# GpSimd work, narrowing steps and gate steps placed anew around the half experts of an attention, mixture and feed-forward kernel

## The chip, the cores and the metric

One NeuronCore of a Trainium2 chip runs the whole program. The metric is the device time of one execution in microseconds (us); 1 us is 1000 ns. The engines are TensorE (PE in the profile, with its weight loads as PEld), VectorE (DVE), ScalarE (ACT), GpSimd (POOL) and the queue that issues DMAs (SP). Each engine works through its own instructions in the order in which the code writes them.

## The reference

```python
# attention: 2 batches, 8 heads, 768 tokens, 64 wide; a window of 128 and 4 sink tokens
a = softmax(where(keep, q @ k.T / 8, -1e9)); x = a @ v          # x: 1536 x 512
# mixture: 8 experts, w1[e] 512 x 1024, w2[e] 1024 x 512
P = exp(x @ w_gate - max)
for _ in range(8):
    P /= P.sum(1, keepdims=True) + 1e-09
    P /= P.sum(0, keepdims=True) + 1e-09
    P *= N / E
for e in range(E):
    out += P[:, e:e+1] * (maximum(x @ w1[e], 0) @ w2[e])
# last layer: w_in 512 x 2048, w_out 2048 x 512
h = out @ w_in; result = (h - tanh(h)) @ w_out
```

## The kernel before

All products run as three matmuls of float32r halves: an operand is cast to a high half (ScalarE, in `split_step` L588), and a subtraction (L591) leaves the low half. The mixture is cut into 32 **half experts**: 2 batches of 768 tokens times 8 experts times 2 halves of the 1024 inner columns. The code counts them with `u`, from 0 to 31, in the loop of `mixture`, and so does the text.

The order of one half expert is written out by hand in `order`. First come the **first products** (`1a` to `3b`, 14 steps of six 384-column matmuls, a fast scheme with seven factors for each of two quartets a and b), with the steps `g0` and `g1` among them. Then come the **second products**: `g2`, `G0`, `G1`, `G2` (six 512-column matmuls each) and `A3`, `A4`, `A5` (twelve each). Second products of token tile n land in a PSUM tile `pg`; there are three of them, so `A5` writes into the one that `G2` left, after VectorE has added it to the accumulator `xa` (the instruction with the scalar `prob`, L939). That addition is called xa2 below, those of `G0` and `G1` xa0 and xa1, and so on to xa5.

Beside the matmuls, each half expert prepares weights for the next one:

- First weights. GpSimd forms sums of loaded blocks in `st` (`sum_next`, L553, two times four instructions). ScalarE casts them in four parts at `g2`, `G0`, `G1`, `G2`, and VectorE subtracts each part one step later (`pending`). Parts 1 and 3 have 1024 columns, parts 2 and 4 have 768. They go to `w1b`.
- Second weights. ScalarE casts two tiles of 1024 columns at `A3` and `A4`; GpSimd subtracts both at the head of the next half expert (`w2_steps`, `step(G)`), in front of the sums. They go to `w2b`.
- Narrowing. The weights of the last layer are converted in 32 pieces by eight VectorE instructions each (`narrow_piece`, tiles `n`, L686 to L701). A half expert takes up to ten such steps, from `u` = 2 on, not in `u` = 15.
- Gates. The normalisation of P (`gates`) runs in `u` = 0 and 1: each step of the generator is a group of small VectorE instructions with one TensorE product `pc`.

ScalarE copies results of first products out of PSUM (`p1`, `u2`, `u3`, L813) so that later factors can be added there.

Of the kernel before, what the change touches and what calls it, by code (L numbers as in the profile page):

```python
# [12 lines left out]
ALU = mybir.AluOpType  # L13
# [9 lines left out]
NI = S // P  # L23
# [18 lines left out]
class Kernel:  # L42
# [187 lines left out]
    def attention_narrow(self, ctx):  # L230
# [7 lines left out]
        ps_t = ctx.enter_context(tc.tile_pool(name="ps_t", bufs=2, space=PSUM))  # L238
        ps_k = ctx.enter_context(tc.tile_pool(name="ps_k", bufs=1, space=PSUM))
        ps_x = ctx.enter_context(tc.tile_pool(name="ps_x", bufs=1, space=PSUM))  # L240
        units = B * NP
# [130 lines left out]
        inputs = self.first_inputs()  # L372
        load_v(0)
        for t in range(T + 5):
# [32 lines left out]
            if t >= 10 and first:  # L407
                later.extend(x for x in [first.pop(0)()] if x)
            if 29 <= t < 29 + NI:
                self.gate_logits(t - 29, ps_t, "t")  # L410
            if t >= 29 and inputs:
                later.extend(x for x in [inputs.pop(0)()] if x)
# [293 lines left out]
    def gates(self, gp):  # L706
# [16 lines left out]
        for _ in range(8):  # L723
# [4 lines left out]
            yield  # L728
            yield
            pc = self.gate_bank([P, NT, E], "pc")  # L730
# [42 lines left out]
    def mixture(self, ctx, gp):  # L773
# [82 lines left out]
        units = 4 * E  # L856
        order = "1a 2a 5a 6a 1b 7a 2b 4a 5b 3a 6b g0 7b g1 4b 3b g2 G0 G1 G2 A3 A4 A5".split()
        firsts = order[: order.index("3b") + 1]
        pending = []
        for u in range(units):  # L860
# [6 lines left out]
            held = {}  # L867

            for step in w2_steps:
                step(G)  # L870
            w2_steps = []
            if u < units - 1:
                self.sum_next()
                self.sum_next()
            if u == 8:
# [15 lines left out]
            for step in order:  # L891
                kind, n = step[0], step[1]
                if kind in "1234567":
                    product(qa if n == "a" else qb, int(kind))
                    if logits and step in ("1b", "7a", "2b", "4a", "5b", "3a"):
                        self.gate_logits(logits.pop(0), ps_g, "g")
                    if u == 1 and not self.gate_done and step in firsts[:11]:
                        self.gate_bank = lambda shape, name: ps_g.tile(shape, F32, tag="g", name=self.nm(name))
                        next(gates, None)
                        if self.gate_done:  # L900
                            for i in range(NI):
                                V.tensor_scalar(
                                    out=self.acc(0, i), in0=self.acc(0, i), scalar1=prob[:, i, 0:1], scalar2=None,
                                    op0=ALU.mult,
                                )
                    continue
# [12 lines left out]
                if todo:  # L919
                    pending.append(todo.pop(0)())  # L920
                if step in ("A3", "A4"):
                    w2_steps += [x() for x in self.split2_next()]
                if fills and step != "g0" and step != "g1":
                    pending.append(fill(1, fills.pop(0)))
                some_narrow({"g2": 1, "G0": 1, "G1": 1, "G2": 2, "A3": 1, "A4": 2, "A5": 2}.get(step, 0))
                if u == 0:
                    self.gate_bank = lambda shape, name: ps_y.tile(shape, F32, tag="y", name=self.nm(name))
                    next(gates)
                if kind != "g":
                    a = self.acc(b, n)  # L930
                    if u == 0:
                        nc.scalar.copy(out=a, in_=held[n])
                    elif e == 0 and hf == 0:
                        V.tensor_scalar(
# [12 lines left out]
            assert not fills and not x2s  # L947
        assert not todo and next(narrow, 0) == 0
        self.w2_steps = w2_steps

# [18 lines left out]
    def last_layer(self, ctx, gp):  # L969
# [71 lines left out]

        for second in self.w2_steps:
            second(G)
        for s in range(steps + 1):
# [50 lines left out]
```

## Time and profile before

| what | value |
| --- | --- |
| time, median of 3 runs | 1545.88 us (1542.59 to 1546.39) |
| the profiled execution's own time | 1548.05 us |
| its span, first to last instruction | 1546.0 us |
| mean granted TensorE clock, as a share of full speed | 0.978 |
| busy share: PE, DVE, ACT, POOL | 93%, 73%, 46%, 36% |

The profiled execution is one run of the program. Its span lies 2.05 us under its own time, and its own time 2.17 us above the median of the other three. A row of the timeline gives the start in us from the span's start, the length in us, the engine, the source line, the operation with the tiles that it writes and reads, the shapes, how many instructions were merged into the row, and in brackets the idle time of the engine before it with what ended it.

### The profile page before, as it was taken

To read this page: it belongs to the slowest core of one execution; us is meant where nothing else is said; L and a number is where in the kernel's file an instruction comes from. 1 tells how busy PE (TensorE), PEld (TensorE's weight loads), DVE (VectorE), ACT (ScalarE), POOL (GpSimd) and SP (SyncE) were. 2 spreads that over 40 slices of the span, in tenths; PEclk is the share of its full clock that TensorE was granted. 3 is DMA by queue.
4 is the path that set the end of the run, shared out by engine and by line. 5 is a ranking of instruction groups with operands and counts; after the bars stand their busy time and mean duration, and the time that the engine had idled before them with its cause. 6 is when DMAs were issued, how large, how long until landed. Compare 5 with 4: busy or idle time off the path is not lost.

```text
span 1546.0 us, 20170 instructions
## 1 busy us (share of the span) xinstructions
PE 1443.5 (93%) x7367; PEld 1255.4 (81%) x7367; DVE 1123.7 (73%) x1971; ACT 705.5 (46%) x1381; POOL 557.6 (36%) x460
## 2 busy tenths in 40 slices
PE   9998899988999999999899999999889999999999
PEld 6667798877888888888788888888779987888887
DVE  6984867777777776777777777777775567777776
ACT  6985334333333333344333333333333357777775
POOL 1113333444453333335444333334444113344422
PEclk9999999999999999999999999999999999999999
DMA  7322122232322222221232323223212120010001
GB/s 142 80 58 84 55 82 76 88 108 77 100 98 70 101 76 75 96 89 55 77 107 94 104 76 96 75 75 99 99 62 89 56 68 22 21 42 14 1 21 61
DMA packets 141865, 114.76 MB, mean 74 GB/s; under 512 B 43840, under 2 KB 113728, under 8 KB 141760
## 3 DMA queue, kind: packets, MB, share of 16 engines
q1 hardware_dynamic: 141472, 113.42, 24.0%
q8 instruction: 59, 0.97, 0.3%
q14 instruction: 46, 0.38, 0.1%
q10 hardware_dynamic: 288, 0.00, 0.0%
HBM read 101.86 MB, written 11.53 MB: 73 GB/s over the span
## 4 chain that ended last, share of the span: by engine, by line
PE 57%; DVE 26%; ACT 11%; issue 4%; DMA 1%; POOL 1%; SPq 0%; ACTq 0%; POOLq 0%; DVEq 0%
PE pg L747 21%; PE px L832 17%; DVE w1b L591 8%; PE pz L832 6%; PE pa L999 6%; PE py L832 4%; ACT w1b L588 4%; DVE xa L939 3%; DVE n L701 1%; DVE n L692 1%; DVE n L697 1%; ACT h L806 1%; ACT an L297 1%; DVE n L688 1%; DVE h L807 1%
## 5 line engine op out<-in xcount | busy, mean ns | idle before, releaser
L747 PE MATMUL pg<-w2b,h 128*128 128x512 f32 x2880 | 717.3, 402 | 73.2 <-DVE xa L939 65.8
L747 PEld LDWEIGHTS pg<-w2b,h 128*128 128x128 f32 x2880 | 550.0, 193 | 200.9 <-DVE xa L939 76.4
L591 POOL TENSOR_TENSOR w2b<-st,w2b 128x1024 fp32r<-128x1024 f32 x72 | 209.4, 2926 | 660.5 <-PE pg L747 579.0
L553 POOL TENSOR_TENSOR st<-st 128x256 f32<-128x256 f32 x248 | 236.2, 956 | 33.5 <-DMA st<-in_moe_w_dram 14.9
L832 PE MATMUL px<-x7c,w1b 128*128 128x384 f32 x1152 | 233.9, 337 | 10.4 <-ACT u L813 9.1
L832 PEld LDWEIGHTS px<-x7c,w1b 128*128 128x128 f32 x1152 | 204.3, 189 | 19.7 <-ACT u L813 12.3
L813 ACT COPY p<-px 128x384 f32<-128x384 f32 x64 | 30.9, 482 | 359.2 <-PE px L832 359.1
L591 DVE TENSOR_TENSOR w1b<-st,w1b 128x1024 fp32r<-128x1024 f32 x127 | 187.3, 1476 | 2.8 <-ACT w1b L588 1.9
L832 PE MATMUL pz<-x7a,w1b 128*128 128x384 f32 x768 | 150.1, 336 | 0.0
L939 DVE SCALAR_TENSOR_TENSOR xa<-pg,prob,xa 128x512 f32<-128x512 f32 x180 | 133.5, 742 | 12.9 <-PE pg L747 12.9
L817 DVE TENSOR_TENSOR u<-u,pz 128x384 f32<-128x384 f32 x64 | 35.5, 554 | 143.8 <-ACT u L813 143.8
L1021 POOL TENSOR_TENSOR h<-y,h 128x384 fp32r<-128x384 f32 x63 | 75.5, 1198 | 175.7 <-ACT h L1020 175.7
L832 PEld LDWEIGHTS pz<-x7a,w1b 128*128 128x128 f32 x768 | 135.1, 189 | 0.0
L588 ACT CAST w1b<-st 128x1024 fp32r<-128x1024 f32 (+1 forms) x132 | 116.1, 948 | 1.4 <-DMA st<-wf_in 1.4
L813 ACT COPY u<-px 128x384 f32<-128x384 f32 x128 | 61.2, 478 | 103.0 <-PE px L832 102.8
L1010 DVE TENSOR_TENSOR y<-pa,tq 128x384 f32<-128x384 f32 x64 | 35.7, 558 | 66.4 <-ACT th L1008 66.3
L832 PE MATMUL px<-x7a,w1b 128*128 128x384 f32 x384 | 79.9, 343 | 2.3 <-issue 2.3
L806 ACT ACTIVATE h<-py 128x384 fp32r<-128x384 f32 x64 | 31.4, 491 | 109.3 <-DVE py L817 109.3
L832 PE MATMUL py<-x7a,w1b 128*128 128x384 f32 x384 | 79.2, 341 | 0.0
L832 PEld LDWEIGHTS px<-x7a,w1b 128*128 128x128 f32 x384 | 70.7, 195 | 6.1 <-issue 3.0
L999 PE MATMUL pa<-x7a,w1b 128*128 128x384 f32 x384 | 73.3, 343 | 0.0
L588 ACT CAST w2b<-st 128x1024 fp32r<-128x1024 f32 x72 | 72.6, 1050 | 0.0
(155 smaller groups left out, 1891.8 us busy)
## 6 DMA issues: line engine op xcount, KB each, us to landing
st<-in_moe_w_dram SPq DMA_DIRECT2D x128, 256.0 KB, 3.1
st<-in_moe_w_dram SPq DMA_DIRECT2D x64, 512.0 KB, 4.8
n<-in_moe_w_in_dram SPq DMA_DIRECT2D x16, 512.0 KB, 4.7
n<-in_moe_w_out_dram SPq DMA_DIRECT2D x16, 512.0 KB, 4.5
wf_in<-n SPq DMA_DIRECT2D x16, 256.0 KB, 2.2
wf_out<-n SPq DMA_DIRECT2D x16, 256.0 KB, 2.2
st<-wf_in SPq DMA_DIRECT2D x8, 512.0 KB, 3.4
st<-wf_out SPq DMA_DIRECT2D x8, 512.0 KB, 3.6
```

Source lines behind the costliest of these rows:

```text
L553: self.nc.gpsimd.tensor_tensor(out=out, in0=a, in1=b, op=op)
L588: self.nc.scalar.copy(out=hi, in_=src)
L591: (engine or self.nc.vector).tensor_tensor(out=lo, in0=src, in1=hi.bitcast(F32), op=ALU.subtract)
L747: self.nc.tensor.matmul(ps, lhsT=self.h[:, f, zh, n * P : (n + 1) * P], rhs=w2[f // 2][:, zw, f % 2, :], start=start and m == 0, stop=stop ...
L806: nc.scalar.activation(out=h[:, f, 0, tok], in_=src, func=AF.Relu)
L813: nc.scalar.copy(out=t, in_=ps)
L817: V.tensor_tensor(out=out, in0=t, in1=ps, op=ALU.add)
L832: nc.tensor.matmul(ps, lhsT=q.w[:, sw, zw, kk * P : (kk + 1) * P], rhs=x[:, zx, kk], start=k in (1, 2, 5) and m == 0, stop=m == 5, skip_gr ...
L939: V.scalar_tensor_tensor(out=a, in0=held[n], scalar=prob[:, b * NI + n, e : e + 1], in1=a, op0=ALU.mult, op1=ALU.add)
L999: nc.tensor.matmul(ps, lhsT=w[:, zw, kk, f % 2 * P : (f % 2 + 1) * P], rhs=x[zx][:, kk], start=m == 0, stop=m == 3 * KD - 1,)
L1010: V.tensor_tensor(out=y, in0=ps, in1=tq, op=ALU.mult)
L1021: engine.tensor_tensor(out=ht[:, 1], in0=y, in1=ht[:, 0].bitcast(F32), op=ALU.subtract)
```

## The change

In the mixture, the first of the two casts of second weights moves from `A3` of the half expert before to the head of the half expert that uses them, and the second to a place behind the first product `1a`; each is followed by its GpSimd subtraction, and the sums of the next first weights follow behind both. The subtraction of the fourth part of the first weights goes from VectorE to GpSimd, at the head of the next half expert (`deferred`). The ten narrowing steps come one at a time: two among the first products (`5b`, `3a`), two at `g0` and `g1`, six from `G0` to `A5`, none at `g2`. The gates take 11 steps where they took 19, at 13 named places of `u` = 0 and 1. The accumulator gathers `u` = 1 without weights and is multiplied by the gates at the head of `u` = 2. In the attention, the first gate logits come every second step, and the fills of the first inputs start one step later and leave out two steps.

```diff
-            if 29 <= t < 29 + NI:
-                self.gate_logits(t - 29, ps_t, "t")
-            if t >= 29 and inputs:
+            if 29 <= t < 29 + 2 * NI and t % 2:
+                self.gate_logits((t - 29) // 2, ps_t, "t")
+            if t >= 30 and t not in (38, 39) and inputs:
...
             V.tensor_tensor(out=prob, in0=prob, in1=rs.unsqueeze(2).to_broadcast([P, NT, E]), op=ALU.mult)
             yield
-            yield
...
-        pending = []
+        pending, deferred = [], []
+        gate_steps = {0: "g2 G0 G1 A3 A4 A5", 1: "6a 2b 3a g1 G1 A3 A4"}
...
+            if deferred:
+                deferred.pop()(G)
+            if u:
+                w2_steps = [step() for step in self.split2_next()]
             for step in w2_steps:
                 step(G)
-            w2_steps = []
-            if u < units - 1:
-                self.sum_next()
-                self.sum_next()
+            if u == 2:
+                for i in range(NI):
+                    V.tensor_scalar(
+                        out=self.acc(0, i), in0=self.acc(0, i), scalar1=prob[:, i, 0:1], scalar2=None, op0=ALU.mult
+                    )
...
-                    if u == 1 and not self.gate_done and step in firsts[:11]:
+                    if step == "1a":
+                        if u:
+                            for x in self.split2_next():
+                                x()(G)
+                        if u < units - 1:
+                            self.sum_next()
+                            self.sum_next()
+                    if step in gate_steps.get(u, "").split():
...
+                    if step in ("5b", "3a"):
+                        some_narrow(1)
                     continue
...
                 if todo:
-                    pending.append(todo.pop(0)())
-                if step in ("A3", "A4"):
-                    w2_steps += [x() for x in self.split2_next()]
+                    (pending if len(todo) > 1 or u == units - 1 else deferred).append(todo.pop(0)())
...
-                some_narrow({"g2": 1, "G0": 1, "G1": 1, "G2": 2, "A3": 1, "A4": 2, "A5": 2}.get(step, 0))
-                if u == 0:
+                if step != "g2":
+                    some_narrow(1)
+                if step in gate_steps.get(u, "").split():
...
+                    elif u == 1:
+                        V.tensor_tensor(out=a, in0=held[n], in1=a, op=ALU.add)
```

VectorE in the second products of one half expert, before, from the step `g2` to xa2 (L939 is the addition to `xa`, L591 the subtraction for `w1b`, the tiles `n` belong to the narrowing):

```order
1553 L694 TENSOR_SCALAR n_8418<-n_8417 128x512
1554 L591 TENSOR_TENSOR w1b<-st_0_70,w1b 128x4x256
1555 L697 SCALAR_TENSOR_TENSOR n_8416<-n_8180,n_8418 128x512
1556 L939 SCALAR_TENSOR_TENSOR xa_65<-pg_8546,prob,xa_65 128x512
1557 L591 TENSOR_TENSOR w1b<-st_0_70,w1b 128x3x256
1558 L699 TENSOR_TENSOR n_8416<-n_8416,n_8417 128x512
1559 L939 SCALAR_TENSOR_TENSOR xa_65<-pg_8564,prob,xa_65 128x512
1560 L591 TENSOR_TENSOR w1b<-st_1_71,w1b 128x4x256
1561 L701 SCALAR_TENSOR_TENSOR n_8418<-n_8180,n_8416 128x512
1562 L686 TENSOR_SCALAR n_8631<-n_8414 128x512
1563 L939 SCALAR_TENSOR_TENSOR xa_65<-pg_8588,prob,xa_65 128x512
1564 L591 TENSOR_TENSOR w1b<-st_1_71,w1b 128x3x256
```

The same place of the changed kernel, where L947 is the addition to `xa`:

```order
1578 L591 TENSOR_TENSOR w1b<-st_0_70,w1b 128x4x256
1579 L690 TENSOR_SCALAR n_8809<-n_8808 128x512
1580 L947 SCALAR_TENSOR_TENSOR xa_65<-pg_8799,prob,xa_65 128x512
1581 L591 TENSOR_TENSOR w1b<-st_0_70,w1b 128x3x256
1582 L692 SCALAR_TENSOR_TENSOR n_8809<-n_8808,n_8809 128x512
1583 L947 SCALAR_TENSOR_TENSOR xa_65<-pg_8823,prob,xa_65 128x512
1584 L591 TENSOR_TENSOR w1b<-st_1_71,w1b 128x4x256
1585 L694 TENSOR_SCALAR n_8810<-n_8809 128x512
1586 L947 SCALAR_TENSOR_TENSOR xa_65<-pg_8848,prob,xa_65 128x512
```

Two of the five narrowing steps ahead of xa2 are gone from here, and the fourth subtraction for `w1b`, which stood behind xa2, has left the engine.

ScalarE at the end of one half expert, before (L588 is the cast, L806 the last activation of the first products):

```order
771 L806 ACTIVATE h<-pz_8522 128x384
772 L588 CAST w1b<-st_0_70 128x4x256
773 L588 CAST w1b<-st_0_70 128x3x256
774 L588 CAST w1b<-st_1_71 128x4x256
775 L588 CAST w1b<-st_1_71 128x3x256
776 L588 CAST w2b_5266<-st_0_5268 128x1024
777 L588 CAST w2b_5267<-st_1_5269 128x1024
```

The same place of the changed kernel, where L812 is the copy of the first product `1a` of the next half expert:

```order
774 L588 CAST w1b<-st_1_71 128x4x256
775 L588 CAST w1b<-st_1_71 128x3x256
776 L588 CAST w2b_5266<-st_0_5268 128x1024
777 L812 COPY p_1394_8696<-px_8689 128x384
778 L588 CAST w2b_5267<-st_1_5269 128x1024
```

The first cast of second weights has no other instruction of its engine between itself and the last cast of first weights, as before; only the second one now stands behind the copy.

GpSimd, one half expert before (L553 are the sums):

```order
126 L591 TENSOR_TENSOR w2b_5266<-st_0_5268,w2b_5266 128x1024
127 L591 TENSOR_TENSOR w2b_5267<-st_1_5269,w2b_5267 128x1024
128 L553 TENSOR_TENSOR st_0_70<-st_0_70 128x256 x4
129 L553 TENSOR_TENSOR st_1_71<-st_1_71 128x256 x4
```

One half expert of the changed kernel on the same engine:

```order
130 L591 TENSOR_TENSOR w1b<-st_1_71,w1b 128x3x256
131 L591 TENSOR_TENSOR w2b_5266<-st_0_5268,w2b_5266 128x1024
132 L591 TENSOR_TENSOR w2b_5267<-st_1_5269,w2b_5267 128x1024
133 L553 TENSOR_TENSOR st_0_70<-st_0_70 128x256 x4
134 L553 TENSOR_TENSOR st_1_71<-st_1_71 128x256 x4
```

The subtraction for `w1b` came in ahead of the two for `w2b`.

## Rows read from the trace of the kernel before

**Rows 1.** Page, part 1: busy us (share of the span) xinstructions of each engine.

```profile
PE 1443.5 (93%) x7367; PEld 1255.4 (81%) x7367; DVE 1123.7 (73%) x1971; ACT 705.5 (46%) x1381; POOL 557.6 (36%) x460
```

**Rows 2.** Waits: engine, line, waited for: total us, times, longest us.

```profile
PE pg L747 <- DVE xa L939: 65.8, 25, 2.9
...
PE px L832 <- ACT u L813: 9.1, 10, 2.5
```

**Rows 3.** Timeline of PE, end of half expert 12 and start of 13.

```profile
582.93 11.08 PE L747 MATMUL pg<-w2b,h 128*128 128x512 f32 x48
596.85 4.60 PE L747 MATMUL pg<-w2b,h 128*128 128x512 f32 x12 [2.83 <-DVE xa L939]
```

**Rows 4.** Windows: window, length, busy us (x) of five engines, PEclk, DMA.

```profile
188.00:190.00 2.00, 1.42 (x9) 1.45 (x10) 1.41 (x5) 0.87 (x2) 0.00 (x0) 1.00 0.00 0
...
599.00:600.00 1.00, 1.00 (x4) 0.81 (x3) 0.97 (x3) 0.00 (x0) 0.12 (x1) 0.50 1.07 344
```

**Rows 5.** Timeline of DVE, second products of half expert 12.

```profile
586.33 0.69 DVE L697 SCALAR_TENSOR_TENSOR n<-n,n 128x512 f32<-128x512 uint16 x1
586.93 0.74 DVE L939 SCALAR_TENSOR_TENSOR xa<-pg,prob,xa 128x512 f32<-128x512 f32 x1
587.60 0.95 DVE L591 TENSOR_TENSOR w1b<-st,w1b 128x768 fp32r<-128x768 f32 x1
...
589.72 2.76 DVE L591 TENSOR_TENSOR w1b<-st,w1b 128x1024 fp32r<-128x1024 f32 x1
592.41 2.86 DVE L701 SCALAR_TENSOR_TENSOR n<-n,n 128x512 int32<-128x512 int32 x1
...
596.06 0.74 DVE L939 SCALAR_TENSOR_TENSOR xa<-pg,prob,xa 128x512 f32<-128x512 f32 x1
```

**Rows 6.** Timeline of POOL, the same stretch.

```profile
588.60 6.12 POOL L591 TENSOR_TENSOR w2b<-st,w2b 128x1024 fp32r<-128x1024 f32 x2 [20.57 <-PE pg L747]
594.68 4.45 POOL L553 TENSOR_TENSOR st<-st 128x256 f32<-128x256 f32 x4
```

**Rows 7.** Timeline of PE, `2a` at the starts of half experts 0, 2, 15, 16, 29, 30.

```profile
132.75 1.57 PE L832 MATMUL py<-x7a,w1b 128*128 128x384 f32 x6
214.75 1.20 PE L832 MATMUL py<-x7a,w1b 128*128 128x384 f32 x6
671.28 1.20 PE L832 MATMUL py<-x7a,w1b 128*128 128x384 f32 x6
703.22 1.20 PE L832 MATMUL py<-x7a,w1b 128*128 128x384 f32 x6
1163.21 1.20 PE L832 MATMUL py<-x7a,w1b 128*128 128x384 f32 x6
1194.23 1.20 PE L832 MATMUL py<-x7a,w1b 128*128 128x384 f32 x6
```

**Rows 8.** Timeline of half expert 29: PE, DVE, ACT, POOL in the second products.

```profile
1179.52 13.80 PE L747 MATMUL pg<-w2b,h 128*128 128x512 f32 x60
...
1181.78 1.22 DVE L591 TENSOR_TENSOR w1b<-st,w1b 128x1024 fp32r<-128x1024 f32 x1 [0.38 <-ACT w1b L588]
...
1180.70 3.45 ACT L588 CAST w1b<-st 128x1024 fp32r<-128x1024 f32 x4
...
1194.42 0.48 ACT L813 COPY p<-px 128x384 f32<-128x384 f32 x1 [8.37 <-PE px L832]
...
1185.18 6.47 POOL L591 TENSOR_TENSOR w2b<-st,w2b 128x1024 fp32r<-128x1024 f32 x2 [21.60 <-PE pg L747]
1191.62 6.32 POOL L553 TENSOR_TENSOR st<-st 128x256 f32<-128x256 f32 x8
```

**Rows 9.** A group of POOL, by form: busy us, mean ns, idle before.

```profile
L591 POOL TENSOR_TENSOR w1b<-st,w1b 128x1024 fp32r<-128x1024 f32 x5 | 12.0, 2403 | 0.0
```

**Rows 10.** Timeline of PE, gate products at the border of half experts 0 and 1.

```profile
173.26 0.43 PE L731 MATMUL pc<-prob,ones 128*128 128x96 f32 x2 [2.01 <-DVE prob L727]
...
188.58 0.43 PE L731 MATMUL pc<-prob,ones 128*128 128x96 f32 x2 [1.79 <-DVE prob L727]
```

More of the change, by code (lines that the diff above doesn't have):

```diff
@@ L857, in mixture @@
         order = "1a 2a 5a 6a 1b 7a 2b 4a 5b 3a 6b g0 7b g1 4b 3b g2 G0 G1 G2 A3 A4 A5".split()
-        firsts = order[: order.index("3b") + 1]
-        pending = []
+        pending, deferred = [], []
+        gate_steps = {0: "g2 G0 G1 A3 A4 A5", 1: "6a 2b 3a g1 G1 A3 A4"}
         for u in range(units):
@@ L896, in mixture @@
                         self.gate_logits(logits.pop(0), ps_g, "g")
-                    if u == 1 and not self.gate_done and step in firsts[:11]:
+                    if step == "1a":
[6 more added lines that the diff above has]
+                    if step in gate_steps.get(u, "").split():
                         self.gate_bank = lambda shape, name: ps_g.tile(shape, F32, tag="g", name=self.nm(name))
                         next(gates, None)
[L900 to L905, printed above, removed]
+                    if step in ("5b", "3a"):
+                        some_narrow(1)
                     continue
@@ L919, in mixture @@
                 if todo:
-                    pending.append(todo.pop(0)())
-                if step in ("A3", "A4"):
-                    w2_steps += [x() for x in self.split2_next()]
+                    (pending if len(todo) > 1 or u == units - 1 else deferred).append(todo.pop(0)())
                 if fills and step != "g0" and step != "g1":
                     pending.append(fill(1, fills.pop(0)))
-                some_narrow({"g2": 1, "G0": 1, "G1": 1, "G2": 2, "A3": 1, "A4": 2, "A5": 2}.get(step, 0))
-                if u == 0:
+                if step != "g2":
+                    some_narrow(1)
+                if step in gate_steps.get(u, "").split():
                     self.gate_bank = lambda shape, name: ps_y.tile(shape, F32, tag="y", name=self.nm(name))
-                    next(gates)
+                    next(gates, None)
                 if kind != "g":
@@ L947, in mixture @@
             assert not fills and not x2s
-        assert not todo and next(narrow, 0) == 0
-        self.w2_steps = w2_steps
+        assert not todo and not deferred and next(narrow, 0) == 0
     def x2(self, b, c):
@@ L1040, in g2_unit @@
                     nc.sync.dma_start(out=self.out[r0 : r0 + P, c0:c1], in_=a[:, c0:c1])
-        for second in self.w2_steps:
-            second(G)
+        for _ in range(2):
+            for step in self.split2_next():
+                step()(G)
         for s in range(steps + 1):
```

## The prediction

> **What bounds the kernel now.** I read the page first. TensorE is busy for 93% of the span, GpSimd for 36% [rows 1]: the end is set by TensorE, and what can be won is its idle time and the time in which its clock is low. The waits say who causes the idle time: TensorE waits 65.8 us in 25 pieces for VectorE's additions to `xa`, 2.6 us each; its wait for ScalarE's copies is 9.1 us in all [rows 2].
>
> So I looked at one such wait. In half expert 12 the second products start at 582.93; `g2` to `A4`, 48 matmuls, take 11.08 us, and then TensorE stands still for 2.83 us until xa2 has freed the tile for `A5` [rows 3]. The twelve matmuls of `A5` should take a quarter of 11.08, 2.8 us, but take 4.60: the granted clock is 0.50, the lower of its two levels, in that stretch [rows 4], after the wait. One wait thus cost some 4.6 us.
>
> Why is xa2 late? VectorE is full: addition and subtraction run back to back. And some of its instructions are far longer than usual. A subtraction of 1024 columns takes 1.22 us [rows 8] but 2.76 here; a narrowing instruction of two inputs takes 0.69 but 2.86. Both fall on the time from 588.60 to 594.72 in which GpSimd subtracts for `w2b` [rows 5, 6], while the additions, which have one input in PSUM, stay at 0.74. The two engines take turns: the VectorE subtraction that starts at 589.72 waits for GpSimd's first instruction, GpSimd's second waits for it, and the narrowing step waits for that one.
>
> What a half expert costs without the trouble stands in the same trace. The narrowing is used up after `u` = 28. From 1163.21 to 1194.23, half expert 29, it takes 31.02 us [rows 7], and its 60 matmuls run through in 13.80 us without a stop [rows 8], with both GpSimd subtractions still there. From `u` = 2 to 28 without 15 (which narrows nothing), 948.46 - 31.94 = 916.5 us go to 26 half experts [rows 7], 35.25 each. **The excess is 4.23 us a half expert, 110 us in all.** This is the pot.
>
> **The change part by part.** I count from T, the start of `g2`, and walk VectorE's queue to xa2 in the new order. Durations are steps from one start to the next.
>
> - *GpSimd's moved work does not start later.* The name of the change says that GpSimd works beside the first products only. The order says otherwise: the first cast of second weights still stands right behind the last cast of first weights on ScalarE, and ScalarE is idle there until the copy of `1a` (idle for 8.37 us before it [rows 8]). In half expert 29 the four casts start at T + 1.2 and end at T + 4.6; GpSimd began at T + 5.7, when the first cast of second weights was done [rows 8]. In the new order the subtraction of part 4 needs only the last of the four casts, so GpSimd starts at T + 4.7, a little earlier than before. Its length: 2403 ns for 1024 columns [rows 9], so about 1.7 us for 768 (an estimate by columns). Then comes the first subtraction for `w2b`, 2.3 to 2.4 us. The second now waits for a cast behind the copy of `1a`, so it and the eight sums leave the second products.
> - *The walk.* Part 1 is subtracted from T + 2.3 [rows 8] to 3.4. One narrowing step (0.4 to 0.6 us, [rows 5] less the overlap) and xa0 (0.66, 586.93 to 587.60 [rows 5]) bring VectorE to T + 4.5 to 4.7, where part 2 (0.9) just precedes GpSimd. GpSimd then holds from 5.4 to 7.1; the narrowing step at `G1` waits and ends at 7.5 to 7.8; GpSimd takes its second turn to 9.8 or 10.1; xa1, which does not wait, ends at 8.2 to 8.5 (`A4` wants it at 8.3). Part 3 waits, and ends at 10.9 to 11.3; a last narrowing step and xa2 end at 12.0 to 12.6. `A5` could start at T + 11.0 (13.80 less its own fifth, 2.76 [rows 8]). **The wait left over is 1.0 to 1.5 us.** The same walk over the old order gives 2.5 to 3.2 where the trace has 2.6 on average, so I take 0.3 off: 1.0 us.
> - *The clock.* A wait of 1.79 us before a gate product [rows 10] left the granted clock at 1.00 [rows 4]. I take no clock loss for waits of 1.0; if it fell each time, it would cost 1.8 us a half expert as above.
> - *The first products.* They get two narrowing steps at `5b` and `3a`, two more at `g0` and `g1`, one subtraction for `w2b` and all eight sums. The cover is VectorE's and ScalarE's slack while TensorE does its 17.3 us there (one step of 1.0 before 1163.21 [rows 7], to 1179.52 [rows 8]). GpSimd's work ends at about 1.7 (copy) + 1.1 (cast) + 2.4 + 6.3 (eight sums [rows 8]) = 11.5 us after the start, and its next reader, the first cast of first weights, comes 18.5 us after it: 7 us of room, of which taking turns may use 3. Queued behind a held VectorE instruction is the next `h` or copy, for which TensorE waits now and then (9.1 us in all [rows 2]). I take 0.1 us a half expert.
> - *The DMAs.* The load of the next block for `st_1` now waits on SP's queue for GpSimd at T + 7 and the second load of second weights for GpSimd 5 us into the next half expert; narrowing loads stand behind. Their data is wanted a whole half expert later (the sums of `st_1` excepted, which have some 10 us), so nothing; if that cover went, SP would hold up the narrowing by a piece, not TensorE.
> - So 26 x (4.23 - 1.0 - 0.1) = 81 us. The longest wait for a copy, 2.5 us [rows 2], lies at the border of 15 and 16, behind seven fills that stay; with it about 3 us stay, which leaves 78.
> - *The gates.* Half experts 0 and 1 take 82.0 us [rows 7], 20 more than 2 x 31.0; gate logits, the cold start and waits share these 20. Waits for gate products of 2.01 and 1.79 us [rows 10] are typical. With two or more matmul steps between gate steps to hide one chain of nine small VectorE instructions, I choose 7 us less, three or four such waits, and 1.5 us back for six multiplications of the accumulator in front of VectorE's first addition of `u` = 2. Bounds: 0 and 10. Net 5.5.
> - *The attention.* The same logits and fills, spread; nothing waits for them before the loop's end. 0, bounds -2 and 2.
>
> Sum: 78 + 5.5 = 83.5. From the profiled execution, 1548.05 - 83.5 = 1464.5; the median of the runs is 2.2 lower, so **1463**.
>
> One row and one rule about the moved subtraction. On VectorE part 4 stood behind xa2, so taking it away makes xa2 no earlier; on GpSimd it adds a turn of 1.7 us in front of xa2. Without it the walk has GpSimd start only at T + 5.7 and take one turn, and xa2 comes at 10.0 to 10.6, before `A5` wants it. So this one part costs the 1.0 us that I leave, 26 us. The Trainium skill, "Perfetto Trace Analysis", section "Optimizing Scalar/DVE Operations", says that moving work between VectorE and GpSimd may not help, since GpSimd reads through a port of VectorE. By that rule the part brings nothing; the lengthened instructions of [rows 5] agree, and the sum stays as it is.
>
> **The rivals.**
>
> - *A. Nothing is left of the wait.* For it: half expert 29 had both subtractions of `w2b` and no wait; the walk has only a few tenths of a microsecond on each side of a turn. Against: the walk. Then 26 x 4.13 = 107, less 3, plus 5.5: 1548 - 110 - 2 = 1436.
> - *B. The turns fall badly.* If GpSimd's first turn comes before part 2 (they ask within 0.2 us of each other, T + 4.5 to 4.7 against 4.7), part 2 ends at 7.3, the narrowing step waits to 10.2, xa1 ends at 10.9, and `A4` waits 2.6 us in the place of `A5`, with the low clock behind half of the waits (0.9 us on average). The gain shrinks to 26 x 0.7 = 18 plus 5.5: about 1522. For it: the small margin, and with a long narrowing step before xa0 they ask at the same time. Against: with a short one VectorE is first, and half of the eight kinds are short.
> - The Trainium skill, "SBUF — State Buffer", section "Who interferes with whom", says that the order of issue decides which of the two blocks, not the kind of operation. By that rule B hangs on the 0.2 us, and the turns in [rows 5, 6] agree.
> - *C. Slower.* The sums come too late. If taking turns in the first products costs GpSimd more than the 7 us of room, the first cast waits, and each further microsecond stops TensorE for one. It is slower than before from 7 + 3.1 = 10 us of delay on; at 11 us it costs 26 us, less the 5.5: about 1566. Against it: GpSimd's eight sums took 6.32 us beside first products [rows 8], and of VectorE's eleven instructions there only two, with both inputs outside PSUM, take turns; with four narrowing steps it is six.
> - *D. The mixture stays and only the gates gain*, if each turn saved is lost again at 7a, where TensorE waits for ScalarE's copies: 1546 - 5.5 = 1540, or within 0.3%. The 9.1 us of such waits [rows 2] speak against it.
>
> **How the numbers follow.** Forecast 0.63, with its own range 1450 to 1482 (0.5 to 1.7 us left in each half expert). A 0.17, B 0.13, C 0.04, D 0.03. From A's 1436 to part of B, 1436 to 1492 holds 8 in 10. About 0.3% (5 us) is what a measurement of this kernel tells from no change. Faster: 0.63 + 0.17 + 0.13 = 0.93; same 0.03; slower 0.04.
>
> **What would show it.** The wait of `A5` for xa2 at about 1 us in the timeline, half experts of 32.1 us; GpSimd's subtraction for `w1b` starting some 4.7 us after `g2`; long VectorE instructions only between T + 5 and T + 11 and, short ones, in the first products; no low clock after `A5`. Wrong if GpSimd is idle in the second products (A), if `A4` waits (B), or if the first cast at `g2` waits for a sum (C).

## The result, and the profile after

The changed kernel takes 1476.74 us (median of 4 runs, 1474.66 to 1479.33), the kernel before 1546.14 (4 runs, 1542.59 to 1547.09): ratio 0.9556, interval 0.9534 to 0.9578. The forecast was 1463, its range 1436 to 1492. So the sign and the range held; of the 83.5 us some 69 came. The profiled execution took 1477.22 us, its span is 1474.7 us and its mean granted clock 0.995 (0.978 before). The two profiled spans differ by 71.3 us, since the profiled execution of before was 2 us above its median.

The page of the changed kernel, part 1 and the main group of part 5, and of its waits the line that answers to [rows 2]:

```profile
PE 1423.6 (97%) x7367; PEld 1232.7 (84%) x7367; DVE 1038.5 (70%) x1940; ACT 704.9 (48%) x1381; POOL 564.5 (38%) x491
...
L746 PE MATMUL pg<-w2b,h 128*128 128x512 f32 x2880 | 705.8, 395 | 28.4 <-DVE xa L947 19.6
```

```profile
PE pg L746 <- DVE xa L947: 19.6, 32, 1.5
```

VectorE is still waited for, even more often than before, but 0.6 us at a time where [rows 2] have 2.6. VectorE's busy time fell by 85 us: 31 subtractions left the engine, and of the narrowing instructions, as many as before, fewer are stretched.

The timeline of TensorE gives the starts of `2a` in half experts 0, 2, 15, 16 and 29, which answer to [rows 7]:

```profile
131.16 1.20 PE L831 MATMUL py<-x7a,w1b 128*128 128x384 f32 x6
215.59 1.20 PE L831 MATMUL py<-x7a,w1b 128*128 128x384 f32 x6
637.37 1.20 PE L831 MATMUL py<-x7a,w1b 128*128 128x384 f32 x6
669.05 1.20 PE L831 MATMUL py<-x7a,w1b 128*128 128x384 f32 x6
1091.59 1.20 PE L831 MATMUL py<-x7a,w1b 128*128 128x384 f32 x6
```

Set against [rows 7], they make a ledger of the two spans:

| stretch | before | after | difference | forecast |
| --- | --- | --- | --- | --- |
| attention, to half expert 0 | 132.75 | 131.16 | -1.6 | 0 |
| half experts 0 and 1 | 82.00 | 84.43 | +2.4 | -5.5 |
| 26 half experts (2 to 28 without 15) | 26 x 35.25 | 26 x 32.47 | -72.2 | -78 |
| half expert 15 | 31.94 | 31.68 | -0.3 | 0 |
| from half expert 29 to the end | 382.8 | 383.1 | +0.3 | 0 |
| sum | 1546.0 | 1474.7 | -71.3 | -83.5 |

Part of the 72.2 us is the clock. Here are the windows of the first 13 of these half experts, before and after (columns as in [rows 4]):

```profile
214.75:671.28 456.53, 419.14 (x2029) 371.98 (x2029) 337.77 (x438) 155.12 (x260) 188.03 (x141) 0.97 0.27 87
```

```profile
215.59:637.37 421.78, 411.05 (x2030) 363.14 (x2030) 301.65 (x435) 154.91 (x260) 189.25 (x151) 1.00 0.30 95
```

The granted clock was 0.97 before and is 1.00 after. Before, `A5` took 1.5 to 2.6 us longer than in half expert 29 in 13 of the 26 half experts, and at most 0.2 longer in the others; after, never more than 0.2. That is some 20 of the 72.2 us, and the rest is shorter waits.

Half expert 13, the one behind that of [rows 3, 5, 6], shows what is left. TensorE, VectorE and GpSimd in its second products (T = 588.93):

```profile
588.93 11.34 PE L746 MATMUL pg<-w2b,h 128*128 128x512 f32 x48
600.91 3.06 PE L746 MATMUL pg<-w2b,h 128*128 128x512 f32 x12 [0.65 <-DVE xa L947]
```

```profile
593.32 0.95 DVE L591 TENSOR_TENSOR w1b<-st,w1b 128x768 fp32r<-128x768 f32 x1
594.19 2.33 DVE L692 SCALAR_TENSOR_TENSOR n<-n,n 128x512 int32<-128x512 int32 x1
596.45 0.74 DVE L947 SCALAR_TENSOR_TENSOR xa<-pg,prob,xa 128x512 f32<-128x512 f32 x1
597.11 2.75 DVE L591 TENSOR_TENSOR w1b<-st,w1b 128x1024 fp32r<-128x1024 f32 x1
599.78 0.41 DVE L694 TENSOR_SCALAR n<-n 128x512 int32<-128x512 int32 x1
600.12 0.74 DVE L947 SCALAR_TENSOR_TENSOR xa<-pg,prob,xa 128x512 f32<-128x512 f32 x1
```

```profile
574.15 2.40 POOL L591 TENSOR_TENSOR w2b<-st,w2b 128x1024 fp32r<-128x1024 f32 x1 [7.76 <-ACT w2b L588]
576.51 6.98 POOL L553 TENSOR_TENSOR st<-st 128x256 f32<-128x256 f32 x8
593.64 2.33 POOL L591 TENSOR_TENSOR w1b<-st,w1b 128x768 fp32r<-128x768 f32 x1 [10.16 <-ACT w1b L588]
595.93 2.84 POOL L591 TENSOR_TENSOR w2b<-st,w2b 128x1024 fp32r<-128x1024 f32 x1
```

This is the walk of the prediction almost to the tenth. GpSimd starts at T + 4.71 (4.7 forecast). VectorE's part 2 came first and ended at 594.27, so that 0.63 of GpSimd's 2.33 us lie beside it and 1.7 behind it. The narrowing step waits for that, GpSimd's second instruction waits for the narrowing step, part 3 for that one, and xa2 ends at 600.86, T + 11.93 (12.0 to 12.6 forecast). `A5` waits 0.65 us, and `A4` some 0.26 in addition (48 matmuls take 11.34 us against 11.08 in [rows 3]). The clock does not fall behind the wait, where [rows 4] had 0.50. The window that shows it (columns as in [rows 4]):

```profile
602.00:604.00 2.00, 2.00 (x11) 1.66 (x10) 1.97 (x4) 0.00 (x0) 0.00 (x0) 1.00 0.00 0
```

### The profile page after: what moved, and what is told of

Read it like the earlier page. It is cut to its first block, busy times and chain, and to the rows that moved or that the text cites. A ratio compares the mean times of both kernels' runs of the same rounds, so it can differ in the third digit from the quotient of the medians.

```text
span 1474.7 us, 20203 instructions
## 1 busy us (share of the span) xinstructions
PE 1423.6 (97%) x7367; PEld 1232.7 (84%) x7367; DVE 1038.5 (70%) x1940; ACT 704.9 (48%) x1381; POOL 564.5 (38%) x491
## 4 chain that ended last, share of the span: by engine, by line
PE 60%; DVE 23%; ACT 10%; issue 4%; POOL 1%; DMA 1%; SPq 0%; ACTq 0%; POOLq 0%; DVEq 0%
PE pg L746 21%; PE px L831 18%; DVE w1b L591 7%; PE pz L831 7%; PE pa L1006 6%; PE py L831 4%; ACT w1b L588 3%; DVE xa L947 3%; DVE h L806 1%; ACT h L805 1%; ACT an L297 1%; DVE n L697 1%; DVE n L701 1%; DVE pz L816 1%; DVE n L692 1%
## 5 line engine op out<-in xcount | busy, mean ns | idle before, releaser
L746 PE MATMUL pg<-w2b,h 128*128 128x512 f32 x2880 | 705.8, 395 | 28.4 <-DVE xa L947 19.6
L746 PEld LDWEIGHTS pg<-w2b,h 128*128 128x128 f32 x2880 | 534.7, 188 | 160.7 <-DVE xa L947 38.0
L591 POOL TENSOR_TENSOR w2b<-st,w2b 128x1024 fp32r<-128x1024 f32 x72 | 184.8, 2569 | 273.3 <-ACT w2b L588 273.3
L591 POOL TENSOR_TENSOR w1b<-st,w1b 128x768 fp32r<-128x768 f32 (+1 forms) x36 | 84.8, 2357 | 337.6 <-ACT w1b L588 337.6
L553 POOL TENSOR_TENSOR st<-st 128x256 f32<-128x256 f32 x248 | 194.6, 790 | 14.6
L812 ACT COPY p<-px 128x384 f32<-128x384 f32 x64 | 30.7, 480 | 329.4 <-PE px L831 329.4
L591 DVE TENSOR_TENSOR w1b<-st,w1b 128x1024 fp32r<-128x1024 f32 (+1 forms) x96 | 152.0, 1583 | 12.0 <-ACT w1b L588 12.0
L947 DVE SCALAR_TENSOR_TENSOR xa<-pg,prob,xa 128x512 f32<-128x512 f32 x174 | 128.9, 742 | 21.0 <-PE pg L746 20.9
L588 ACT CAST w1b<-st 128x1024 fp32r<-128x1024 f32 (+1 forms) x132 | 116.0, 946 | 1.4 <-DMA st<-wf_in 1.4
L812 ACT COPY u<-px 128x384 f32<-128x384 f32 x128 | 61.3, 479 | 99.9 <-PE px L831 99.9
L805 ACT ACTIVATE h<-pz 128x384 fp32r<-128x384 f32 x64 | 31.5, 492 | 93.8 <-DVE pz L816 93.8
L588 ACT CAST w2b<-st 128x1024 fp32r<-128x1024 f32 x72 | 75.4, 1050 | 0.0
```

Source lines behind the costliest of these rows:

```text
L553: self.nc.gpsimd.tensor_tensor(out=out, in0=a, in1=b, op=op)
L588: self.nc.scalar.copy(out=hi, in_=src)
L591: (engine or self.nc.vector).tensor_tensor(out=lo, in0=src, in1=hi.bitcast(F32), op=ALU.subtract)
L746: self.nc.tensor.matmul(ps, lhsT=self.h[:, f, zh, n * P : (n + 1) * P], rhs=w2[f // 2][:, zw, f % 2, :], start=start and m == 0, stop=stop ...
L805: nc.scalar.activation(out=h[:, f, 0, tok], in_=src, func=AF.Relu)
L812: nc.scalar.copy(out=t, in_=ps)
```

## The experiments

The theory, called turns: an instruction of GpSimd and one of VectorE with both inputs outside PSUM go one after the other; the number of such pairs ahead of xa2 sets how late xa2 is. The main rival, called load: VectorE simply has too much to do ahead of xa2, so what counts is the time of its own work. All half experts below are the mean of the same 26 as in the ledger, and each ratio is to the kernel before, run on the same chip.

**The fourth part back on VectorE**, all else as in the changed kernel:

```diff
-                    (pending if len(todo) > 1 or u == units - 1 else deferred).append(todo.pop(0)())
+                    pending.append(todo.pop(0)())
```

> The changed kernel with one thing undone: the subtraction of part 4 of the first weights stays on VectorE, behind xa2. Theory of turns (the wait of A5 is as long as the GpSimd instructions that VectorE has to let pass ahead of xa2): GpSimd takes only one turn there, starting 1 us later; the wait of 0.6 to 0.9 us goes, half experts of 31.1 to 31.4 us in place of 32.5, so 26 x 1.2 = 31 us faster than the changed kernel, about 1445. Rival, theory of load (the wait is set by how much work VectorE has in the second products): VectorE gets 0.9 us more per half expert, so the same as the changed kernel or up to 10 us slower, 1477 to 1487.

Measured: 1440.53 us (1439.86 to 1443.34), ratio 0.9310 [0.9277, 0.9343], 36 us less than the whole change. A half expert takes 31.24 us. Second products of one (T = 601.87), TensorE, VectorE and GpSimd:

```profile
601.87 13.80 PE L746 MATMUL pg<-w2b,h 128*128 128x512 f32 x60
```

```profile
607.13 0.69 DVE L697 SCALAR_TENSOR_TENSOR n<-n,n 128x512 f32<-128x512 uint16 x1
607.73 0.75 DVE L947 SCALAR_TENSOR_TENSOR xa<-pg,prob,xa 128x512 f32<-128x512 f32 x1
608.39 2.77 DVE L591 TENSOR_TENSOR w1b<-st,w1b 128x1024 fp32r<-128x1024 f32 x1
611.08 0.68 DVE L699 TENSOR_TENSOR n<-n,n 128x512 f32<-128x512 f32 x1
611.68 0.74 DVE L947 SCALAR_TENSOR_TENSOR xa<-pg,prob,xa 128x512 f32<-128x512 f32 x1
```

```profile
607.54 2.53 POOL L591 TENSOR_TENSOR w2b<-st,w2b 128x1024 fp32r<-128x1024 f32 x1 [11.21 <-PE pg L746]
```

One turn instead of two: only part 3 is stretched (2.77), the narrowing step before it keeps its 0.69, xa2 ends at T + 10.55, and the 60 matmuls run through. VectorE has no less work ahead of xa2 than in the changed kernel and more behind it, and TensorE waits less. That speaks for turns.

**The narrowing alone**, in the kernel before (ten steps one by one, as the change has them):

```diff
+                    if step in ("5b", "3a"):
+                        some_narrow(1)
...
-                some_narrow({"g2": 1, "G0": 1, "G1": 1, "G2": 2, "A3": 1, "A4": 2, "A5": 2}.get(step, 0))
+                if step != "g2":
+                    some_narrow(1)
```

> The kernel before with the narrowing spread as in the change, and nothing else of it. Theory of turns: two narrowing steps fewer ahead of xa2, the two GpSimd turns stay; the walk leaves a wait of about 1.4 to 1.7 us, half experts of 32.5 to 33 us, so 60 to 70 us faster than before: 1476 to 1486. Theory of load: four steps of some 0.55 us leave the second products, which takes 2.2 of the 2.6 us of wait and the low clock with it: half experts of 31.5 us, about 1450.

Measured: 1489.11 us (1486.65 to 1492.62), ratio 0.9617 [0.9580, 0.9655], half experts of 32.96, and `A5` still waits for xa2 (the waits, first line):

```profile
PE pg L747 <- DVE xa L942: 37.2, 24, 1.7
```

Both GpSimd subtractions still fall ahead of xa2; what got shorter is the queue between. The half experts lie where turns put them; the time is 3 us above the range given.

**The second weights alone**, in the kernel before (casts, subtractions and sums as the change has them; narrowing, gates and the fourth part untouched):

```diff
+            if u:
+                w2_steps = [step() for step in self.split2_next()]
             for step in w2_steps:
                 step(G)
-            w2_steps = []
-            if u < units - 1:
-                self.sum_next()
-                self.sum_next()
...
+                    if step == "1a":
+                        if u:
+                            for x in self.split2_next():
+                                x()(G)
+                        if u < units - 1:
+                            self.sum_next()
+                            self.sum_next()
...
-                if step in ("A3", "A4"):
-                    w2_steps += [x() for x in self.split2_next()]
...
```

> The kernel before with the casts of second weights, their subtractions and the sums moved as in the change, all ten narrowing steps and part 4 of the first weights where they were. Theory of turns: one GpSimd turn ahead of xa2 in place of two and no sums beside the second products; the walk leaves no wait, half experts of 31.1 to 31.4 us, about 1440 to 1450, faster than the whole change. Theory of load: VectorE keeps all its work, so most of the wait of 2.6 us stays: 1520 to 1545.

Measured: 1455.35 us (1454.91 to 1455.84), ratio 0.9399 [0.9366, 0.9431], half experts of 31.57; the time is 5 us above the range that turns gave, and half experts 0 and 1 took 4 us more than before. VectorE has as many narrowing steps and subtractions ahead of xa2 here as before, and yet the wait is nearly gone:

```profile
PE pg L747 <- DVE xa L942: 4.5, 12, 1.8
```

Load falls with this: VectorE's queue is as it was, only the second of the two subtractions and the sums have left GpSimd's queue beside it, and with them 92 us. It also prices the narrowing: once the second weights have moved, spreading it is worth some (31.57 - 31.24) x 26 = 9 us.

**The gates as before**, all else as in the changed kernel: the old 19 steps, at every step of `u` = 0 that writes `pg` (`g0` and `g1` too) and at the first eleven of `u` = 1, with the accumulator multiplied in `u` = 1.

```diff
...
-                    if step in gate_steps.get(u, "").split():
+                    if u == 1 and not self.gate_done and step in firsts[:11]:
...
-                if step in gate_steps.get(u, "").split():
+                if u == 0:
...
```

> The changed kernel with the gates as before: 19 steps at the places of before, and the accumulator weighted in half expert 1. The two traces give half experts 0 and 1 together 84.4 us with the new gates and 82.0 with the old. If the new places cause that (the last gate chain runs beside the second products of half expert 1 and delays xa2, a wait of 2.43 us there): 2 to 4 us faster than the changed kernel. If the moved GpSimd work causes it and the new gate places help as predicted: 3 to 7 us slower.

Measured: 1478.30 us (1477.65 to 1481.67), ratio 0.9554 [0.9519, 0.9589]: as the whole change, within what can be told apart, so neither expectation came. Half experts 0 and 1 take 84.66 us against 84.43; what lies behind this is taken up below, under the gates.

**The fourth part alone**, in the kernel before:

```diff
...
+            if deferred:
+                deferred.pop()(G)
             for step in w2_steps:
                 step(G)
...
-                    pending.append(todo.pop(0)())
+                    (pending if len(todo) > 1 or u == units - 1 else deferred).append(todo.pop(0)())
```

> The kernel before with only the subtraction of part 4 of the first weights moved to GpSimd. Theory of turns: GpSimd gets a third turn beside the second products, 1 us earlier, and VectorE loses work only behind xa2: the wait of A5 stays or grows by up to 1 us, half experts of 35.0 to 36.5 us, 1540 to 1575. Theory of load: 0.9 us of the 2.6 us of wait goes: 26 x 1 us faster, 1520.

Measured: 1610.75 us (1608.93 to 1611.81), ratio 1.0411 [1.0392, 1.0431], slower, and by more than expected; half experts of 37.44, mean granted clock 0.960. TensorE, VectorE and GpSimd in one of them, and the window behind the wait:

```profile
623.79 4.60 PE L747 MATMUL pg<-w2b,h 128*128 128x512 f32 x12 [3.94 <-DVE xa L941]
```

```profile
613.76 2.34 DVE L699 TENSOR_TENSOR n<-n,n 128x512 f32<-128x512 f32 x1
...
616.69 2.76 DVE L591 TENSOR_TENSOR w1b<-st,w1b 128x1024 fp32r<-128x1024 f32 x1
619.38 2.83 DVE L701 SCALAR_TENSOR_TENSOR n<-n,n 128x512 int32<-128x512 int32 x1
```

```profile
612.95 2.60 POOL L591 TENSOR_TENSOR w1b<-st,w1b 128x768 fp32r<-128x768 f32 x1 [16.10 <-ACT w1b L588]
615.52 6.14 POOL L591 TENSOR_TENSOR w2b<-st,w2b 128x1024 fp32r<-128x1024 f32 x2
```

```profile
626.00:627.00 1.00, 1.00 (x4) 0.75 (x3) 1.00 (x3) 0.00 (x0) 0.00 (x0) 0.50 1.13 325
```

Three turns now: three GpSimd instructions, three stretched VectorE instructions, a wait of 3.94 us, and `A5` at the lower clock behind it. The engine with the work taken off it became later.

**GpSimd's work really beside the first products only.** Two kernels: the first has the fourth part on VectorE and both casts of second weights behind the copy of `1a`; the second is the changed kernel with all GpSimd work behind that copy, the fourth part between the two subtractions for `w2b`.

```diff
-            if deferred:
-                deferred.pop()(G)
-            if u:
-                w2_steps = [step() for step in self.split2_next()]
-            for step in w2_steps:
-                step(G)
+            if not u:
+                for step in w2_steps:
+                    step(G)
...
                                 x()(G)
+                            if deferred:
+                                deferred.pop()(G)
+                            for x in self.split2_next():
+                                x()(G)
+                        elif deferred:
+                            deferred.pop()(G)
```

> As the run with part 4 on VectorE, and both casts of second weights (the subtractions with them) behind the copy of the first product 1a, so that GpSimd has nothing left to do beside the second products. Theory of turns: there was no wait left to remove, so within 3 us of that run, 1438 to 1444. Rival, room in the first products: two casts in a row on ScalarE hold up the activation behind 2a by 1 us, which reaches TensorE at 7a: 0.3 to 1 us per half expert, 8 to 26 us slower than that run.

> The changed kernel with all GpSimd work really beside the first products: both casts of second weights behind the copy of 1a, and the GpSimd subtraction of part 4 of the first weights between the two subtractions for w2b. Theory of turns: the wait of A5 goes as when part 4 is on VectorE; the four subtractions and eight sums then end some 16 us after the start of a half expert, 2 us ahead of the first cast, and turns with the narrowing steps at 5b and 3a cost 0.5 to 0.8 us at 7b: half experts of 31.5 to 31.9 us, 1450 to 1462, still faster than the changed kernel. Rival C of the prediction, the sums come too late: the first cast at g2 waits for a sum and half experts take 33 us or more, 1490 and up.

Measured, the first: 1437.93 us (1437.30 to 1439.12), ratio 0.9298 [0.9282, 0.9315], not told apart from the 1440.53 with the first cast early; most half experts take 31.02, but `u` = 2 35.08 and `u` = 7 33.00. The second: 1469.39 us (1467.08 to 1469.64), ratio 0.9495 [0.9477, 0.9512], half experts of 32.31, some 7 us better than the change as it is, and 7 us above the range expected. Most of its half experts take 31.94, close to the 31.5 to 31.9 expected, but `u` = 2, with its six multiplications, takes 37.78. GpSimd and TensorE of the second, in first products:

```profile
603.94 2.40 POOL L591 TENSOR_TENSOR w2b<-st,w2b 128x1024 fp32r<-128x1024 f32 x1 [18.35 <-ACT w2b L588]
606.29 1.84 POOL L591 TENSOR_TENSOR w1b<-st,w1b 128x768 fp32r<-128x768 f32 x1
608.10 2.40 POOL L591 TENSOR_TENSOR w2b<-st,w2b 128x1024 fp32r<-128x1024 f32 x1
610.46 6.84 POOL L553 TENSOR_TENSOR st<-st 128x256 f32<-128x256 f32 x8
```

```profile
614.85 1.31 PE L831 MATMUL px<-x7c,w1b 128*128 128x384 f32 x6 [0.66 <-ACT u L812]
```

The wait of `A5` is gone, and one of 0.66 us for ScalarE's copy at `7b` has taken its place: in the first products the turns are not free either. The sums end 3 us before the first cast that reads them.

**Gate steps of `u` = 1 at other places** (`1b 4a 6b 4b G0`), with the fourth part on VectorE:

```diff
-        gate_steps = {0: "g2 G0 G1 A3 A4 A5", 1: "6a 2b 3a g1 G1 A3 A4"}
+        gate_steps = {0: "g2 G0 G1 A3 A4 A5", 1: "1b 4a 6b 4b G0"}
...
```

> As the run with part 4 on VectorE, with the gate steps of half expert 1 at 1b, 4a, 6b, 4b and G0 in place of 6a, 2b, 3a, g1 and G1: each gate product then has at least three matmul steps behind the step before, and the small instructions stand ahead of those that wait for a new product. If the waits for gate products come from the places: half experts 0 and 1 together fall from 79.9 to 75 or 76 us, the whole to about 1436. If they come from GpSimd's turns: no change, 1440.

Measured: 1438.65 us (5 runs, 1436.84 to 1439.85), ratio 0.9297 [0.9282, 0.9313]; half experts 0 and 1 take 79.31 us against 79.94, and not the 75 or 76 that better places should have given. These five places are worth nothing that can be told against the seven of the change.

**Second weights subtracted on VectorE**, in the kernel before. Turns say that `A5` stops waiting although VectorE gets 2 x 1.2 us more to do in each half expert; load says that it waits longer.

```diff
                 if step in ("A3", "A4"):
-                    w2_steps += [x() for x in self.split2_next()]
+                    pending += [x() for x in self.split2_next()]
```

> The kernel before with the two subtractions for w2b on VectorE, one step behind their casts, so that GpSimd only makes the sums. VectorE has 2.3 us more work per half expert, all of it behind xa2, and no long turn ahead of it. Theory of turns: the wait of A5 for xa2 disappears altogether, although VectorE does more; what VectorE could not finish holds up the start of the next half expert, so that waits at 7a of up to 3 us appear; half experts of 32 to 34.5 us, 1465 to 1530. Theory of load: the wait of A5 grows, half experts over 36 us, 1570 and more.

Measured: 1518.18 us (1514.32 to 1525.17), ratio 0.9806 [0.9785, 0.9827]. TensorE in second and first products, and its main wait:

```profile
574.47 13.80 PE L747 MATMUL pg<-w2b,h 128*128 128x512 f32 x60
...
595.58 1.32 PE L832 MATMUL px<-x7c,w1b 128*128 128x384 f32 x6 [2.08 <-ACT u L813]
```

```profile
PE px L832 <- ACT u L813: 55.6, 26, 4.5
```

The wait of `A5` vanished with GpSimd's turns, although VectorE runs 64 instructions more than before (2035 against the 1971 of [rows 1]). The gain is small because the two subtractions now stand in front of VectorE's part of the first products, where TensorE waits at `7a`.

**The bundles spread**, from the first kernel with all casts behind the copy: the six multiplications of the accumulator one by one over the first products of `u` = 2, and eight sums of `u` = 8 (`t_sum`) one in each half expert from 3 to 10.

```diff
...
+                    if step == "5b" and 3 <= u < 11:
+                        self.t_sum(1, (u - 3) // 2, (u - 3) % 2, G)
+                    if u == 2 and step in scaled:
+                        i = scaled.index(step)
+                        V.tensor_scalar(
+                            out=self.acc(0, i), in0=self.acc(0, i), scalar1=prob[:, i, 0:1], scalar2=None, op0=ALU.mult
+                        )
...
```

> As the run with both casts behind the copy of 1a and part 4 on VectorE, with two bundles spread: the six multiplications of the accumulator one by one over first products of half expert 2, and the eight GpSimd differences of input blocks one per half expert from 3 to 10 in place of all in 8. That run spends 35.1 us in half expert 2 and 33.0 in 7 in place of 31.0. If the bundles cause it, 5 to 6 us go: about 1432. If not, no change, 1438.

Measured: 1435.69 us (6 runs, 1434.68 to 1447.81), ratio 0.9297 [0.9270, 0.9323]. `u` = 2 fell from 35.08 to 32.91 us and `u` = 7 from 33.00 to 31.01, 4 us in place of the 5 to 6 expected; half experts 0 and 1, the same in both kernels, took 2.1 us more. The expected 1432 was not reached. It is the fastest median of all, though not apart from the 1437.93.

## Why the prediction was right, and where it was off

**The excess and its cause: right, and shown.** Taking GpSimd's turns away, in two different ways, removed the wait of `A5` (all narrowing still there in the one, more VectorE work in the other), and a third turn lengthened it to 3.9 us.

**The walk: right in its steps, a little short in its price.** GpSimd at T + 4.71, xa2 at T + 11.93, no low clock in the 26 half experts. In place of 1.1 us a half expert, 32.47 - 31.02 = 1.45 us were left. The starts of TensorE's steps, averaged over the 26 and held against half expert 29, say where: `A4` starts 0.16 us late, `A5` 1.01 later still, and the `1a` behind it a further 0.15; 0.08 are the wait at `7a` in half expert 16, and 0.05 small waits in other first products. So the 0.1 taken for the first products held. The 1.17 us ahead of `A5` lie inside the walk's own 1.0 to 1.5; what was mis-sized are the 0.3 us taken off it, and the 0.15 behind the wait, for which the sum has no term. A smaller slip is in the walk too: 2403 ns for 1024 columns make 1.8 us for 768 by columns, not 1.7, and 1.84 was measured where no VectorE instruction was in the way (the row at 606.29 above). With half expert 15 all this is 5.5 us less gain than forecast.

**The border: not the fills alone.** Half expert 16 takes 34.82 us. The prediction left about 3 us there to the seven fills. The wait, and the VectorE instruction ahead of it:

```profile
675.38 1.33 PE L831 MATMUL px<-x7c,w1b 128*128 128x384 f32 x6 [2.01 <-ACT u L812]
```

```profile
671.32 2.64 DVE L63 TENSOR_TENSOR x7a<-xa,x7a 128x768 fp32r<-128x768 f32 x1
```

This subtraction of the last fill takes its turn with GpSimd's subtraction for `w2b` (670.75 to 673.15). With both casts behind the copy and the fourth part on VectorE the same subtraction took 0.96 us, and half expert 16, with the same seven fills, 31.02; with the first cast early it took 34.87. So the wait at the border is a turn as well.

**The gates: the step that failed.** "I choose 7 us less, three or four such waits, and 1.5 us back ... Net 5.5." Half experts 0 and 1 got 2.4 us longer. Gate products still wait; the rows answer to [rows 10], and the last is new, an addition held up in the second products of `u` = 1:

```profile
178.00 0.46 PE L730 MATMUL pc<-prob,ones 128*128 128x96 f32 x2 [2.11 <-DVE prob L727]
183.45 0.46 PE L730 MATMUL pc<-prob,ones 128*128 128x96 f32 x2 [1.72 <-DVE prob L727]
188.81 0.46 PE L730 MATMUL pc<-prob,ones 128*128 128x96 f32 x2 [1.72 <-DVE prob L727]
...
208.96 5.73 PE L746 MATMUL pg<-w2b,h 128*128 128x512 f32 x24 [2.43 <-DVE xa L940]
```

The traces split the two half experts, in us. "First" is the time from `2a` to `g2`, "second" from `g2` to the next `2a`:

| kernel | `u` = 0 first | second | `u` = 1 first | second |
| --- | --- | --- | --- | --- |
| before | 23.69 | 18.25 | 25.37 | 14.69 |
| second weights alone | 23.98 | 15.92 | 31.43 | 14.69 |
| gates as before, else the change | 23.88 | 16.52 | 29.57 | 14.69 |
| the whole change | 25.37 | 16.08 | 25.33 | 17.65 |
| fourth part back on VectorE | 23.59 | 16.09 | 23.75 | 16.52 |
| that, and both casts behind the copy | 23.10 | 16.09 | 22.27 | 14.94 |

Kernels with the same code in a stretch differ by up to 1.8 us there (23.59 and 25.37), so small differences say nothing. Two things stand out. In the first products of `u` = 1 the moved second weights put GpSimd beside the old gate steps and cost 4 to 6 us; the new steps take some 4 back (29.57 to 25.33), so against the kernel before nothing is won there. And the new steps put the last gate chain into the second products of `u` = 1. Where no GpSimd instruction runs beside it, this costs 0.25 us (14.94 against 14.69), with one 1.8, with two, as in the change, 3.0. VectorE and GpSimd there:

```profile
204.16 1.53 DVE L732 TENSOR_SCALAR cs<-cs 128x8 f32<-128x8 f32 x1
205.72 0.20 DVE L733 RECIPROCAL cs<-cs 128x8 f32<-128x8 f32 x1
205.96 2.05 DVE L734 TENSOR_SCALAR cs<-cs 128x8 f32<-128x8 f32 x1
```

```profile
203.73 1.94 POOL L591 TENSOR_TENSOR w1b<-st,w1b 128x768 fp32r<-128x768 f32 x1 [19.64 <-ACT w1b L588]
205.62 2.36 POOL L591 TENSOR_TENSOR w2b<-st,w2b 128x1024 fp32r<-128x1024 f32 x1
```

Two instructions that take 0.17 us elsewhere take 1.53 and 2.05, and the addition behind them comes late. They have one input, so turns are wider than the theory as stated. What was left out is that the gates' VectorE work is held up by GpSimd like the rest: the prediction walked through the queue of a half expert from `u` = 2 on, not through that of `u` = 1.

The prediction took no clock loss for waits of 1.0 us, because one wait of 1.79 us had left the clock at 1.00. Behind the third gate wait above the clock did fall:

```profile
190.00:194.00 4.00, 4.00 (x14) 3.44 (x13) 2.45 (x10) 0.70 (x2) 0.00 (x0) 0.57 0.00 0
```

So it had in the kernel before, behind the other wait of [rows 10], of 2.01 us (0.53 from 174 to 181). For the 26 half experts the choice was right.

The 1.5 us for the multiplications in `u` = 2 hardly showed in the changed kernel (half expert 2 takes 0.3 us more than 3), but were 4 and 6 us in a bundle and still 2 one by one where all of GpSimd's work lay beside them.

**The price of the fourth part: right in sign, small in size.** 26 us forecast, 36 measured: (32.47 - 31.24) x 26 = 32 in the half experts, 4.5 in the first two, of which only the 1.1 in the second products of `u` = 1 fall where the fourth part runs. The Trainium skill, "Perfetto Trace Analysis", section "Optimizing Scalar/DVE Operations", says that moving work between VectorE and GpSimd may not help; here it agrees and is mild: alone, the move made the kernel 4.1% slower.

**The parts don't add.** Against the kernel before, the second weights alone gave 92 us, the narrowing alone 59, the fourth part alone -63: 88 together, where the whole gave 69. Second weights and narrowing cure the same wait, and the fourth part costs 36 behind them instead of 63.

**The rivals.** A, nothing left: not in this kernel, but it is what the change becomes without the fourth part. B, the turns fall badly: part 2 started at 593.32, GpSimd at 593.64; the sign named for B, a wait of `A4`, came at 0.26 us, a tenth of B's 2.6. C, the sums too late: they end before 584, and GpSimd then stands idle for 10 us; even with all its work behind the copy 3 us were left. D fell with the 69 us. What the change is called, GpSimd beside the first products only, is not what the kernel does, as the prediction said; making it so is worth 7 us, taking the fourth part back 36.

**Open:** why half experts 0 and 1 differ by up to 2 us between kernels that should be alike there, and why one wait of TensorE is followed by the lower clock and another of the same length is not.

## What to carry to other kernels

Where an engine is late and some of its instructions are far longer than the same instructions elsewhere, ask first what other engine runs beside the long ones; moving that neighbour gave 92 us here, spreading the late engine's own work 59, and handing its work to the neighbour lost 63. Count the turns ahead of the waited-for instruction, since each holds an instruction up for about the neighbour's length. And price a change in the stages where both its parts meet: the gates' gain was real, and GpSimd's moved work, another part of the same change, ate it.

## What the runs showed of the hardware

- The handed-over subtraction of 768 columns took 0.95 us on VectorE and 1.84 on GpSimd where neither was held, but its price to the kernel was set by whom it held up: 63 us over 31 half experts alone, 36 within the change.
- Instructions of VectorE with one input in PSUM kept their 0.74 us beside GpSimd in every run; those with both inputs outside went from 0.69 to 2.3 to 2.9 and from 1.22 to 2.8. With one input, outside PSUM, TENSOR_SCALAR went from 0.17 to 1.53 and 2.05 beside GpSimd, and RECIPROCAL kept its 0.20.
- Behind waits of `A5` of 3.9 us the granted clock showed 0.50, the lower of the two levels, and the twelve matmuls took 4.60 us; behind 0.65 us they took 3.06 at 1.00. A wait of 1.79 us for a gate product left 1.00 before; one of 1.72, the third such wait within 13 us, was followed by a fall (0.57 from 190 to 194 us after).
